# Three units of an expert layer's first product computed by seven half-size products

## The chip, the cores and the metric

One core of one Trainium2 chip runs the kernel. The metric is device time in microseconds (us) of one execution. TensorE (PE) multiplies matrices into PSUM, VectorE (DVE) and ScalarE (ACT) read PSUM and work elementwise, GpSimd (POOL) copies and issues transfers, SyncE (SP) issues transfers. Each engine carries out its own list of instructions in order and waits on semaphores for the others.

## The reference

Attention with a relative-position bias for 8 batches of 8 heads, 576 positions and 64 channels, and then a two-layer network with a squared ReLU on the 4608 tokens that it gives:

```python
scores = scale * np.matmul(q, k.transpose(0, 1, 3, 2)) + bias   # bias_table[bucket], per head
attn = softmax(scores)                                          # over the keys
x = (attn @ v).transpose(0, 2, 1, 3).reshape(B * S, H * D)      # 4608 x 512
h = np.maximum(x @ w_in, 0.0)                                   # w_in: 512 x 2048
out = h * h @ w_out                                             # w_out: 2048 x 512
```

All inputs and the output are fp32; the kernel multiplies in fp16 and accumulates in fp32.

## The kernel before

The kernel makes a list of operations, each with its engines, what it depends on, the ring buffers it takes and a due time (`P.add`), and a planner (`Plan.schedule`) puts them in order by its own cost figures. The order in which the planner lists them is each engine's program order; what an instruction waits for on the chip is then set by the tiles it reads and writes.

The work is of two kinds. **Attention** runs over 32 pairs of heads (`pair`): four score matmuls into the two double-bank PSUM tiles `st` (L702, with L726 and L751 for the last 64 queries and keys), exponentials on ACT from there into a `pt` buffer (L713), a table product on DVE (L794), the product with v into the one PSUM tile `pv` (L830, L837) in two parts, its normalisation on DVE into `x` (L854, L859), and a transposing transfer on SP's queue that puts `x` into `xt` with channels on the partitions (L875). **The two layers** run over nine groups of 512 tokens (`layers`). Layer 1 of a group is 16 tiles, one for each 128 of the 2048 hidden channels: four matmuls of 512 columns over the four 128-channel parts of x into one of three PSUM tiles `f` (L1102), a ReLU on ACT into one of four `rt` buffers (L1123), a square on DVE into the group's `g` buffer (L1133). Layer 2 of a group is computed already by seven half-size products in place of eight (`second`, Winograd's variant of Strassen's scheme): sums of activations on DVE (L972), seven products of 16 matmuls of 256 columns each, issued as two halves of eight (L1017), sums with the products on DVE or a plain copy on ACT (L1045, L1051), and the output transfers on SP (L1073).

In the list a group's 16 layer-1 tiles are due 2000 apart, and the halves of the layer-2 products of the group before lie between them. Groups 7 and 8 take tokens of the last batch (7), so that their layer 1 comes after the last pair (31); after that pair there are no more scores, and the two `st` tiles, the `pt` buffers and the staging buffers of q and k (`stg`, shown as qs and ks) are no longer used. Group 8 has no group after it: its layer 2 is the end of the kernel.

Of the kernel before, what the change touches and what calls it, by code (L numbers as in the profile page):

```python
# [11 lines left out]
FP16 = mybir.dt.float16  # L12
EXPF = mybir.ActivationFunctionType.Exp
RELUF = mybir.ActivationFunctionType.Relu
COPYF = mybir.ActivationFunctionType.Copy
MULT = mybir.AluOpType.mult

# [8 lines left out]
GT = 512  # L26
# [13 lines left out]
SIX = 2  # L40
V_EARLY, V_HW = 18900.0, 2
LATE2 = 7000
T_POOL, T_DUE = 0, 0
ORDER = "k0 i0 q1 q0 v i1 o0 k1 i2 o1 o2 i3 o3"
HALF = GT // 2
# [135 lines left out]
def mm(n):  # L181
    return n / 2.4 + 2.5
# [6 lines left out]
def dve(n, rate=1.0, fix=160.0):  # L189
    return fix + n / (0.96 * rate)  # L190
# [3 lines left out]
def kernel(  # L194
# [13 lines left out]
    def io(ins):  # L208
        tc.keep_in_program_order(ins)
        return ins  # L210
# [399 lines left out]

    xt_ready, x_last = {}, {}
    x_bufs = {}

    def copy_to(engs_n, out_f, in_f, deps, bufs, due, fp16=True, dve_only=False):

# [13 lines left out]
    def pair(p):  # L629
# [63 lines left out]
        def run(jts):  # L693
            sets = [Buf(r_set) for _ in jts]

            def score():
                kt, qt = kts[qb.slot], qts[qb.slot]
                for jt, st in zip(jts, sets):
                    for e in range(2):
                        rw = ds(64 * e, 64)  # L700
                        io(
                            nc.tensor.matmul(  # L702
                                sets_ps[st.slot][:, e, :], kt[rw, ts(jt, 128)], qt[rw, 0:512],
                                start=True, stop=True,
                            )
                        )

            o = P.add({"PE": len(jts) * mm(512) + 10}, score, evac, sets + [qb, pb], T, after, "r")
            for jt, st in zip(jts, sets):

                def ex(jt=jt, st=st):
                    io(
                        nc.scalar.activation(  # L713
                            out=p5(pts[pb.slot])[:, jt, :, 0:512], in_=sets_ps[st.slot], func=EXPF, scale=SCALE
                        )
                    )

                exps[jt] = P.add({"ACT": act(1024)}, ex, [o], [st, pb], T)
# [214 lines left out]
    def sums_of_weights():  # L933
# [21 lines left out]
            done.append(o)  # L955
        return done

    def sums_of_activations(g):

        gb = g_bufs[g]  # L960
        sb_ = s_bufs[g] = {i: Buf(r_s[i]) for i in (1, 2, 4)}
        for c0 in (0, 4):
            o = None
            for to, uses in ((1, [1]), (2, [1, 2]), (4, [2, 4]), (3, [])):

                def add(to=to, c0=c0):
                    a11, a12, a21, a22 = (fourth(gb, eo, t, c0, 4) for t in range(2) for eo in range(2))
                    s = {i: ss[i][:, c0 : c0 + 4] for i in (1, 2, 4)}
                    out_, a, b_ = {
                        1: (s[1], a21, a22), 2: (s[2], a11, s[1]), 4: (s[4], a12, s[2]), 3: (a21, a21, a11)  # L970
                    }[to]
                    io(nc.vector.tensor_tensor(out=out_, in0=a, in1=b_, op=mybir.AluOpType.subtract))  # L972

                o = P.add(
                    {"DVE": dve(1024, 2.0)}, add, squares[g][2 * c0 : 2 * c0 + 8] + [o],
                    [gb] + [sb_[i] for i in uses], G0 + GP * g - 5e4,
                )
                s_done.setdefault((g, to), []).append(o)

    def second(g):  # L980
# [25 lines left out]
        for i in (int(x) for x in (P_LAST if g == NG - 1 else P_ORDER).split()):  # L1006
            bk, left, right, ns = prod[i]
            own = bk == "e" and g == NG - 1
            home = pv_ps if own else g_ps
            apart = bk == "d" and g == NG - 1  # L1010
            for s_ in range(2):
                bf = bank[f"d{s_}" if bk == "d" else bk]

                def mul(i=i, s_=s_, bf=bf, left=left, right=right, apart=apart, own=own, home=home):
                    for c in range(8):
                        io(
                            nc.tensor.matmul(  # L1017
                                home[bf.slot][:, ts(s_, HALF)], left(c, s_), right(c),
                                start=(c == 0 and (s_ == 0 or apart) and (own or i not in before)), stop=(c == 7),
                                skip_group_check=True,  # L1020
                            )
                        )

                def atom(d, i=i, s_=s_, bf=bf, ns=ns, mul=mul, own=own):
                    deps = d + [x for n in ns for x in s_done[g, n]] + squares[g]
                    deps += read_of[before[i]] if i in before and not own else []
                    deps += l_wout if i in (1, 2) else t_done
                    return P.add(
                        {"PE": 8 * mm(HALF)}, mul, deps, [bf, gb] + [sb_[n] for n in ns if n != 3], 1e6, 0.0, "f",
                    )  # L1030

                atoms.append(atom)
                if s_ == 0 and not apart:
                    continue

                def fin(o, i=i, bf=bf, s0=s_ if apart else 0, n=1 if apart else 2, own=own, home=home):
                    to, plus, where = reads[i]
                    plus = "u" if own else plus
                    cs = ds(s0 * HALF, n * HALF)

                    def ev():
                        dst, ps = ys[y[to].slot][:, cs], home[bf.slot][:, cs]
                        if plus is not None:
                            io(
                                nc.vector.scalar_tensor_tensor(  # L1045
                                    out=dst, in0=ps, scalar=OSC, in1=ys[y[plus].slot][:, cs], op0=MULT,
                                    op1=mybir.AluOpType.add,
                                )
                            )
                        elif e.eng == "ACT":  # L1050
                            io(nc.scalar.activation(out=dst, in_=ps, func=COPYF, scale=OSC))  # L1051
                        else:
                            io(nc.vector.tensor_scalar_mul(out=dst, in0=ps, scalar1=OSC))

                    deps = [o]
                    if plus == "u":
                        deps += read_of[1 if i in (2, 6) else 6]
                    if i == 6 and g == NG - 1:
                        deps += read_of[2]
                    if plus == "v":  # L1060
                        deps += read_of[5]
                    if i == 4:
                        deps += read_of[3] + read_of[5]
                    bufs = [bf, y[to]] + ([y[plus]] if plus not in (None, to) else [])
                    engs = {"DVE": dve(n * HALF)} if plus is not None else {"DVE": dve(n * HALF), "ACT": act(n * HALF)}
                    e = P.add(engs, ev, deps, bufs, 0.0)
                    read_of.setdefault(i, []).append(e)
                    if where is not None:
                        t, h = where
                        P.add(  # L1070
                            {"SP": 640.0},
                            lambda: io(
                                nc.sync.dma_start(  # L1073
                                    out=rows_[t][:, s0 : s0 + n, ts(h, HALF)],
                                    in_=ys[y[to].slot][:, cs].rearrange("p (s d) -> p s d", s=n),
                                )
                            ),
                            [e], [y[to]], 0.0,
                        )

                atoms.append(fin)
        return atoms

    def layers(g):

        due = G0 + GP * g
# [2 lines left out]
        if g < NG:  # L1089
            g_bufs[g] = Buf(r_gb)  # L1090
            gb1 = g_bufs[g]
            squares[g] = []
            for nt in range(16):
                bank = Buf(r_g)

                def f1(nt=nt, bank=bank):
# [10 lines left out]
                            )  # L1107

                atoms1.append((nt, f1, bank))
        i2 = 0  # L1110
        last = None
        for i in range(16):
            if i < len(atoms1):
                nt, f1, bank = atoms1[i]
                o = P.add(
                    {"PE": 4 * mm(512)}, f1, xt_ready[g] + [l_win[nt // 4]], [bank, gb1], due + i * 2000, 0.0, "f"
                )
                f1_last[g] = o
                rb = Buf(r_rt)
# [1 line left out]
                def relu(o, bank=bank, rb=rb):  # L1121
# [4 lines left out]

                engs = {"ACT": act(512), "DVE": dve(512)} if g < RELU_DVE else {"ACT": act(512)}
                r = one_of(engs, relu, [o], [bank, rb], 0.0)
                squares[g].append(
                    P.add(  # L1130
                        {"DVE": dve(512, 2.0)},
                        lambda rb=rb, nt=nt, gb1=gb1: io(
# [64 lines left out]
```

## Time and profile before

| what | value |
|---|---|
| median of 7 runs | 373.34 us (372.69 to 374.43) |
| the profiled execution's own time | 373.06 us |
| its span, first to last instruction | 371.2 us |
| ACT busy, 300-310 / 310-315 / 315-320 us | 4.43 / 0.00 / 2.26 us |
| DVE busy, 300-310 / 310-315 / 315-320 us | 7.05 / 2.81 / 1.91 us |
| DVE busy, 320-325 / 325-330 / 330-335 us | 3.05 / 4.11 / 4.36 us |
| DVE busy, 335-340 / 340-345 / 345-350 / 350-355 us | 1.36 / 1.88 / 3.34 / 2.83 us |
| layer-1 matmuls of groups 7 and 8 | 314.13 us to 355 us |
| last matmuls begin | 366.21 us |

A profile is of one execution. In a timeline each line is a start, a length, the engine, the line of the kernel, the operation, what it writes and reads, the shape and the count of merged instructions; in brackets the idle time of the engine before it and what ended that. The page's slices cut the span into 40; a digit is the busy share in tenths. Matmuls are pipelined, so that the length of one is longer than the distance to the next.

### The profile page before, as it was taken

What the parts mean: (1) busy time and instruction counts of PE and PEld (TensorE: products, weight loads), DVE (VectorE), ACT (ScalarE), POOL (GpSimd) and SP (SyncE); (2) the same over time, 40 slices, a digit from 0 to 9 for tenths busy, and PEclk for the clock granted to TensorE, in tenths of its full rate; (3) what the DMA queues carried; (4) which work ended last, traced back from release to release, by engine and by line L of the source; (5) the groups of instructions that cost most, each with busy time, mean ns of one, the idle gap of its engine ahead of it and who ended that gap; (6) DMA issues with size and microseconds to landing.
All of it is one profiled execution on the core that took longest, in us unless ns stands there. A gap on an engine that the chain in (4) does not pass through costs nothing.

```text
span 371.2 us, 9910 instructions
## 1 busy us (share of the span) xinstructions
PE 355.2 (96%) x3930; PEld 242.4 (65%) x3930; DVE 265.1 (71%) x594; ACT 257.5 (69%) x367; POOL 188.2 (51%) x343
## 2 busy tenths in 40 slices
PE   3988999899999999999999999999999999999996
PEld 2756455556587457877785467745876688546785
DVE  3997789967775598668865787579765885583573
ACT  4998989688576887679766887688659870564220
POOL 7898349494665687668755655677623100000000
PEclk9999999999999999999999999999999999999999
DMA  9999999895999999999999799999975112200022
GB/s 166 151 133 160 201 179 87 108 112 99 174 127 127 149 161 116 150 164 156 116 132 148 115 140 133 135 170 142 121 107 130 48 44 57 78 2 28 30 85 87
DMA packets 162292, 44.25 MB, mean 119 GB/s; under 512 B 145734, under 2 KB 162246, under 8 KB 162246
## 3 DMA queue, kind: packets, MB, share of 16 engines
q0 software_dynamic: 74208, 14.53, 50.4%
q1 hardware_dynamic: 87696, 28.80, 41.0%
q8 instruction: 31, 0.51, 0.6%
q10 hardware_dynamic: 342, 0.30, 0.3%
q14 instruction: 15, 0.12, 0.1%
HBM read 36.88 MB, written 9.44 MB: 125 GB/s over the span
## 4 chain that ended last, share of the span: by engine, by line
PE 86%; DVE 7%; DMA 3%; ACT 2%; issue 1%; POOL 0%; SPq 0%; ACTq 0%; DVEq 0%
PE f L1102 34%; PE f L1017 28%; PE pv L837 8%; PE st L702 8%; PE pv L830 2%; PE st L751 2%; DVE pt L794 2%; DMA kt<-ks 2%; PE st L726 1%; DVE x L859 1%; DMA g<-in_q_dram 1%; PE f L657 1%; ACT pm L761 1%; DVE s L972 1%; PE f L359 1%
## 5 line engine op out<-in xcount | busy, mean ns | idle before, releaser
L713 ACT ACTIVATE pt<-st 128x1024 f16<-128x1024 f32 x128 | 127.4, 1024 | 30.7 <-PE st L702 30.7
L1102 PE MATMUL f<-xt,w_in_sb 128*128 128x512 f16 (+4 forms) x704 | 138.5, 341 | 0.2 <-ACT xt L619 0.2
L1123 ACT ACTIVATE rt<-f 128x512 f16<-128x512 f32 x144 | 85.2, 601 | 49.2 <-PE f L1102 44.0
L1102 PEld LDWEIGHTS <-w_in_sb 128*128 128x128 f16 x704 | 62.5, 98 | 57.3 <-issue 12.2
L1133 DVE TENSOR_TENSOR g<-rt 128x512 f16<-128x512 f16 x144 | 64.0, 449 | 36.3 <-ACT rt L1123 35.1
L794 DVE TENSOR_TENSOR pt<-pt,tb_sb 128x1536 f16<-128x1536 f16 (+2 forms) x96 | 60.6, 641 | 14.7 <-ACT pt L713 14.0
L1017 PEld LDWEIGHTS <-g 128*128 128x128 f16 x576 | 54.5, 98 | 14.4 <-issue 4.7
L276 POOL DMA_DIRECT2D qs<-in_q_dram x79 | 55.4, 714 | 7.4 <-DMA w_in_sb<-in_moe_w_in_dram 2.5
L276 POOL DMA_DIRECT2D ks<-in_k_dram x79 | 55.3, 702 | 1.1 <-issue 1.0
L837 PE MATMUL pv<-va,pt 128*128 128x65 f16 x1280 | 54.7, 193 | 0.0
L837 PEld LDWEIGHTS <-pt 128*128 128x128 f16 x1280 | 50.2, 97 | 3.2 <-issue 1.3
L1045 DVE SCALAR_TENSOR_TENSOR y<-f,y 128x512 f32<-128x512 f32 (+1 forms) x47 | 31.4, 667 | 23.1 <-PE f L1017 22.7
L1017 PEld LDWEIGHTS <-s 128*128 128x128 f16 x432 | 41.2, 98 | 9.8 <-issue 2.5
L702 PE MATMUL st<-qt,kt 64*128 64x512 f16 x256 | 40.5, 387 | 0.9 <-ACT pt L736 0.4
L684 POOL COPY qz<-kt 64x64 f16<-64x64 f16 x58 | 21.1, 364 | 38.8 <-DMA kt<-ks 31.9
L830 PE MATMUL pv<-vm,pm 128*128 128x130 f16 x160 | 35.3, 221 | 1.1 <-DVE x L859 1.0
L1017 PE MATMUL f<-wt,g 128*128 128x256 f16 x288 | 36.2, 273 | 0.0
L1017 PE MATMUL f<-w_out_sb,s 128*128 128x256 f16 x288 | 36.1, 273 | 0.0
L684 POOL COPY qz<-qt 64x64 f16<-64x64 f16 x61 | 18.4, 302 | 33.1 <-DMA qt<-qs 29.7
L1017 PE MATMUL f<-w_out_sb,g 128*128 128x256 f16 x272 | 34.5, 273 | 0.7 <-ACT y L1051 0.7
L859 DVE TENSOR_TENSOR x<-pv,r 128x384 f16<-128x384 f32 x64 | 31.4, 491 | 2.0
L972 DVE TENSOR_TENSOR s<-g,s 128x1024 f16<-128x1024 f16 x36 | 25.1, 698 | 0.4
(66 smaller groups left out, 285.7 us busy)
## 6 DMA issues: line engine op xcount, KB each, us to landing
out_dram<-y SPq DMA_DIRECT2D x34, 256.0 KB, 2.3
f<-in_v_dram SPq DMA_DIRECT2D x24, 256.0 KB, 4.2
qs<-in_q_dram POOLq DMA_DIRECT2D x48, 64.0 KB, 4.3
ks<-in_k_dram POOLq DMA_DIRECT2D x48, 64.0 KB, 3.7
w_in_sb<-in_moe_w_in_dram POOLq DMA_DIRECT2D x4, 512.0 KB, 8.9
w_out_sb<-in_moe_w_out_dram POOLq DMA_DIRECT2D x4, 512.0 KB, 12.8
qs<-in_q_dram POOLq DMA_DIRECT2D x7, 144.0 KB, 4.3
ks<-in_k_dram POOLq DMA_DIRECT2D x7, 144.0 KB, 6.7
```

Source lines behind the costliest of these rows:

```text
L276: lambda: io(eng.dma_start(out=out_(), in_=in_())),
L684: io(eng.tensor_copy(out=dst[qb.slot][rw, rw], in_=src[qb.slot][rw, 512:576]))
L702: nc.tensor.matmul(sets_ps[st.slot][:, e, :], kt[rw, ts(jt, 128)], qt[rw, 0:512], start=True, stop=True,)
L713: nc.scalar.activation(out=p5(pts[pb.slot])[:, jt, :, 0:512], in_=sets_ps[st.slot], func=EXPF, scale=SCALE)
L794: io(nc.vector.tensor_tensor(out=a, in0=a, in1=t, op=MULT))
L830: nc.tensor.matmul(ps[:, i, :, :], pm[:, c : c + 128], vm[:, hp, :, 0:65], start=True, stop=False)
L837: nc.tensor.matmul(ps[:, i, e, :], pt[:, (2 * jt + e) * S + c : (2 * jt + e) * S + c + 128], va[:, jt, 2 * hp + e, 0:65], start=False, sto ...
L859: nc.vector.tensor_tensor(out=xs[xb.slot][:, qt0 : qt0 + nq, :].rearrange("p t (e d) -> p t e d", e=2), in0=ps[:, :, :, 0:64], in1=rs[rb.s ...
L1017: nc.tensor.matmul(home[bf.slot][:, ts(s_, HALF)], left(c, s_), right(c), start=(c == 0 and (s_ == 0 or apart) and (own or i not in before ...
L1102: nc.tensor.matmul(g_ps[bank.slot][:, a:z], w_in_sb[:, kk, ts(nt, 128)], xt_sb[:, kk, c : c + z - a], start=(kk == 0), stop=(kk == 3),)
L1123: io(nc.scalar.activation(out=rts[rb.slot], in_=g_ps[bank.slot], func=RELUF))
L1133: nc.vector.tensor_tensor(out=gs[gb1.slot][:, nt, :], in0=rts[rb.slot], in1=rts[rb.slot], op=MULT)
```

## The change

`UNITS` names two units of group 7 and one of group 8. A unit is four layer-1 tiles: hidden channels 256u to 256u + 255 and 1024 + 256u to 1024 + 256u + 255. They are no longer computed tile by tile. `by_sevens` takes the block of w_in and the group's part of xt as 2x2 blocks (halves of the hidden channels, halves of the 512 input channels, halves of the 512 tokens) and computes the four result blocks by seven products of four matmuls of 256 columns, in place of eight. Products 1, 6, 2 go to one `st` tile (1 and 2 to its first bank, 6 to its second), 5, 7, 3, 4 to the other (5 and 3 to the first, 7 and 4 to the second). ACT copies product 1 to an fp32 buffer (one of the two `f32` buffers), DVE adds the others to what has been made so far, from PSUM; the four results go through ReLU (on ACT) and square (on DVE or ACT) into `g`.

The sums of blocks of xt (four for each group) are made on DVE into staging buffers; the sums of blocks of w_in (four for each unit u, made once) on DVE into a `pt` buffer, with the scores of the last pair as something they depend on and the due time of group 7. The other tiles of the group get due times between those of the seven products (`place`, `AT`). The list `squares` is kept by tile, so that a sum of activations depends on its own tiles.

```diff
+UNITS = {7: 2, 8: 1}
+
+AT = (0, 0.5, 2, 2.5, 4, 5.5, 7)
...
+    last_scores = []
             o = P.add({"PE": len(jts) * mm(512) + 10}, score, evac, sets + [qb, pb], T, after, "r")
+            if p == 4 * B - 1:
+                last_scores.append(o)
...
+    def made(g, a, z):
+
+        return [x for nt in range(a, z) for x in squares[g][nt]]
-                    {"DVE": dve(1024, 2.0)}, add, squares[g][2 * c0 : 2 * c0 + 8] + [o],
+                    {"DVE": dve(1024, 2.0)}, add, made(g, 2 * c0, 2 * c0 + 8) + [o],
-                    deps = d + [x for n in ns for x in s_done[g, n]] + squares[g]
+                    deps = d + [x for n in ns for x in s_done[g, n]] + made(g, 0, 16)
...
+    def sum_of_w(i, u):
+        return pts[late["room"].slot][:, ts(i - 1, 1024)].rearrange("p (k c) -> p k c", k=2)[:, :, ts(u, 256)]
...
+    def by_sevens(g, units, due):
...
+
+            late["room"] = Buf(r_pt)
+        wq = lambda i, k, u: w_in_sb[:, 2 * k : 2 * k + 2, 1024 * i + 256 * u : 1024 * i + 256 * u + 256]
+        xq = lambda k, j: xt_sb[:, 2 * k : 2 * k + 2, c + HALF * j : c + HALF * j + HALF]
+        o_ = 4 * (g - min(UNITS)) - 1
+        t = lambda i: stg[(i + o_) // 2][(i + o_) % 2][:, 0:512].rearrange("p (k c) -> p k c", k=2)
+        t_ops = late_sums(
+            512, t,
+            [
+                (1, (lambda: xq(0, 1), lambda: xq(0, 0), SUB)),
+                (2, (lambda: xq(1, 1), lambda: t(1), SUB)),
+                (4, (lambda: xq(1, 0), lambda: t(2), SUB)),
+                (3, (lambda: xq(1, 1), lambda: xq(0, 1), SUB)),
+            ],
+            xt_ready[g], due - 1e5,
+        )
+        gb1 = g_bufs[g]
...
+        for u in range(units):
+            s_ = lambda i, u=u: sum_of_w(i, u)
+            if ("ops", u) not in late:
+                late["ops", u] = late_sums(
+                    512, s_,
+                    [
+                        (1, (lambda u=u: wq(1, 0, u), lambda u=u: wq(1, 1, u), mybir.AluOpType.add)),
+                        (2, (lambda s_=s_: s_(1), lambda u=u: wq(0, 0, u), SUB)),
+                        (4, (lambda u=u: wq(0, 1, u), lambda s_=s_: s_(2), SUB)),
+                        (3, (lambda u=u: wq(0, 0, u), lambda u=u: wq(1, 0, u), SUB)),
+                    ],
+                    l_win + last_scores, due + 10.0 * u, [late["room"]],
+                )
+            sets = {"ab": Buf(r_set), "cd": Buf(r_set)}
+            y = {"u": Buf(r_f), "v": Buf(r_y)}
+            at = lambda i, y=y: (fs if i == "u" else ys)[y[i].slot]
+            prod = {
+                1: ("a", lambda u=u: wq(0, 0, u), lambda: xq(0, 0), True),
+                6: ("b", lambda s_=s_: s_(2), lambda: t(2), True),
+                2: ("a", lambda u=u: wq(0, 1, u), lambda: xq(1, 0), False),
+                5: ("c", lambda s_=s_: s_(1), lambda: t(1), True),
+                7: ("d", lambda s_=s_: s_(3), lambda: t(3), True),
+                3: ("c", lambda s_=s_: s_(4), lambda: xq(1, 1), False),
+                4: ("d", lambda u=u: wq(1, 1, u), lambda: t(4), False),
+            }
+            reads = {
+                1: ("u", None, None), 6: ("u", "u", None), 2: (None, None, (0, 0)), 5: ("v", "u", None),
+                7: (None, "v", (1, 1)), 3: (None, "u", (0, 1)), 4: (None, "u", (1, 0)),
+            }
+            after_read = {2: 1, 3: 5, 4: 7}
+            read_of = {}
+            for n, i in enumerate((1, 6, 2, 5, 7, 3, 4)):
+                bk, left, right, first_ = prod[i]
+                st = sets["ab" if bk in "ab" else "cd"]
+                ps = lambda st=st, bk=bk: sets_ps[st.slot][:, "abcd".index(bk) % 2, :]
+
+                def mul(left=left, right=right, first_=first_, ps=ps):
+                    for f in range(2):
+                        for kk in range(2):
+                            io(
+                                nc.tensor.matmul(
+                                    ps()[:, ts(f, HALF)], left()[:, kk, ts(f, 128)], right()[:, kk, :],
+                                    start=(first_ and f == 0 and kk == 0), stop=(kk == 1), skip_group_check=True,
+                                )
+                            )
+
+                o = f1_last[g] = P.add(
+                    {"PE": 4 * mm(HALF)}, mul,
+                    xt_ready[g] + t_ops + late["ops", u] + (read_of[after_read[i]] if i in after_read else []),
+                    [st, gb1, late["room"]], due + (8 * u + AT[n]) * 2000.0, 0.0, "f",
+                )
+                to, plus, where = reads[i]
+                deps = [o]
+                if plus == "u":
+                    deps += read_of[1 if i == 6 else 6]
+                if plus == "v":
+                    deps += read_of[5]
+                bufs = [st] + [y[x] for x in {to, plus} - {None}]
+                rb = Buf(r_rt) if where else None
+                bufs += [rb] if rb else []
+
+                def ev(e, to=to, plus=plus, ps=ps, at=at, rb=rb):
+                    dst = rts[rb.slot] if rb else at(to)
+                    if plus is not None:
+                        io(
+                            nc.vector.scalar_tensor_tensor(
+                                out=dst, in0=ps(), scalar=1.0, in1=at(plus), op0=MULT, op1=mybir.AluOpType.add
+                            )
+                        )
+                    else:
+                        io(nc.scalar.activation(out=dst, in_=ps(), func=RELUF if rb else COPYF))
+
+                e = one_of({"DVE": dve(512) + 100.0} if plus else {"ACT": act(512) + 100.0}, ev, deps, bufs, 0.0)
+                read_of[i] = [e]
+                if not rb:
+                    continue
+                if plus is not None:
+                    e = P.add(
+                        {"ACT": act(512)},
+                        lambda rb=rb: io(nc.scalar.activation(out=rts[rb.slot], in_=rts[rb.slot], func=RELUF)),
+                        [e], [rb], 0.0,
+                    )
+
+                def square(o, rb=rb, where=where, u=u):
+                    src = rts[rb.slot].rearrange("p (f s) -> p f s", f=2)
+                    n0 = 8 * where[0] + 2 * u
+                    dst = gs[gb1.slot][:, n0 : n0 + 2, ts(where[1], HALF)]
+                    if o.eng == "ACT":
+                        io(nc.scalar.activation(out=dst, in_=src, func=SQUAREF))
+                    else:
+                        io(nc.vector.tensor_tensor(out=dst, in0=src, in1=src, op=MULT))
+
+                e = one_of({"DVE": dve(512, 2.0), "ACT": act(512)}, square, [e], [rb, gb1], due - 1e5)
+                for f in range(2):
+                    squares[g][8 * where[0] + 2 * u + f].append(e)
...
-            squares[g] = []
-            for nt in range(16):
+            squares[g] = {nt: [] for nt in range(16)}
+            units = UNITS.get(g, 0)
+            for nt in [nt for nt in range(16) if nt % 8 >= 2 * units]:
                 bank = Buf(r_g)
                 atoms1.append((nt, f1, bank))
+            if units:
+                by_sevens(g, units, due)
+
+            def place(d):
+                return 2 * d + 1 if d < 4 * units else 4 * units + d
+
+        skip = 16 - len(atoms1) if g < NG else 0
-            if i < len(atoms1):
-                nt, f1, bank = atoms1[i]
+            if i >= skip and g < NG:
+                nt, f1, bank = atoms1[i - skip]
                 o = P.add(
-                    {"PE": 4 * mm(512)}, f1, xt_ready[g] + [l_win[nt // 4]], [bank, gb1], due + i * 2000, 0.0, "f"
+                    {"PE": 4 * mm(512)}, f1, xt_ready[g] + [l_win[nt // 4]], [bank, gb1], due + place(i - skip) * 2000,
+                    0.0, "f",
                 )
...
-                squares[g].append(
+                squares[g][nt].append(
```

More of the change, by code (lines that the diff above doesn't have):

```diff
@@ L14 @@
 RELUF = mybir.ActivationFunctionType.Relu
+SQUAREF = mybir.ActivationFunctionType.Square
 COPYF = mybir.ActivationFunctionType.Copy
@@ L1082, in second, with late_sums @@
         return atoms
+    late = {}
+    def sum_of_w(i, u):
+        return pts[late["room"].slot][:, ts(i - 1, 1024)].rearrange("p (k c) -> p k c", k=2)[:, :, ts(u, 256)]
+    def late_sums(n, dst, terms, deps, due, bufs=()):
+        o, made_ = None, []
+        for i, (a, b_, op) in terms:
+            o = P.add(
+                {"DVE": dve(n, 2.0)},
+                lambda i=i, a=a, b_=b_, op=op: io(nc.vector.tensor_tensor(out=dst(i), in0=a(), in1=b_(), op=op)),
+                deps + [o], bufs, due,
+            )
+            made_.append(o)
+        return made_
@@ new lines @@
+    SUB = mybir.AluOpType.subtract
+    def by_sevens(g, units, due):
+        assert max(UNITS.values()) <= 2
+        if not late:
+            late["room"] = Buf(r_pt)
+        c = (g * GT) % XR
+        assert c + GT <= XR
+        wq = lambda i, k, u: w_in_sb[:, 2 * k : 2 * k + 2, 1024 * i + 256 * u : 1024 * i + 256 * u + 256]
[90 more added lines that the diff above has]
+                        [e], [rb], 0.0,
+                    )
+                def square(o, rb=rb, where=where, u=u):
[9 more added lines that the diff above has]
+                    squares[g][8 * where[0] + 2 * u + f].append(e)
```

## The prediction

> **What bounds the kernel now.** I read the page's busy and slice rows first, then the timelines of TensorE (PE), VectorE (DVE) and ScalarE (ACT) over the last 75 us, where the edit lies.
>
> ```profile
> PE 355.2 (96%) x3930; PEld 242.4 (65%) x3930; DVE 265.1 (71%) x594; ACT 257.5 (69%) x367; POOL 188.2 (51%) x343
> PE   3988999899999999999999999999999999999996
> ...
> PEclk9999999999999999999999999999999999999999
> ```
>
> The page's busy rows and slices: PE is full to the last slice, at full clock.
>
> ```profile
> 315.87 1.89 PE L1102 MATMUL f<-xt,w_in_sb 128*128 128x512 f16 x8
> 317.60 1.04 PE L1017 MATMUL f<-wt,g 128*128 128x256 f16 x8
> 318.47 14.84 PE L1102 MATMUL f<-xt,w_in_sb 128*128 128x512 f16 x68
> 333.15 1.04 PE L1017 MATMUL f<-w_out_sb,g 128*128 128x256 f16 x8
> 334.02 1.03 PE L1102 MATMUL f<-xt,w_in_sb 128*128 128x512 f16 x4
> 334.88 1.04 PE L1017 MATMUL f<-w_out_sb,g 128*128 128x256 f16 x8
> ...
> 366.21 1.91 PE L1017 MATMUL f<-wt,g 128*128 128x256 f16 x16
> ```
>
> PE's timeline (start, length, instruction; durations run past the next start, so only differences of starts count). From 296 us on there is no gap. 68 matmuls of 512 columns take 333.15 - 318.47 = 14.68 us: 0.8635 a layer-1 tile of four. Eight of 256 columns take 0.873 (333.15 to 334.02): four would take 0.4365. So here a microsecond of matmul saved or lost is one of the end, if PE stays full.
>
> ```profile
> 314.13 1.03 PE L1102 MATMUL f<-xt,w_in_sb 128*128 128x512 f16 x4
> 315.00 1.04 PE L1017 MATMUL f<-wt,g 128*128 128x256 f16 x8
> 315.20 0.60 ACT L1123 ACTIVATE rt<-f 128x512 f16<-128x512 f32 x1 [9.34 <-PE f L1102]
> 315.83 0.43 DVE L1133 TENSOR_TENSOR g<-rt 128x512 f16<-128x512 f16 x1 [0.80 <-ACT rt L1123]
> ```
>
> All engines, the first tile of group 7: its matmuls give way at 315.00, ACT starts at 315.20 (hand-over 0.20), ends at 315.80, DVE starts at 315.83 (0.03).
>
> ```profile
> 314.33 0.69 DVE L1045 SCALAR_TENSOR_TENSOR y<-f,y 128x512 f32<-128x512 f32 x1 [1.06 <-PE f L1017]
> 18.59 0.56 DVE L859 TENSOR_TENSOR x<-pv,r 128x384 f16<-128x384 f32 x1
> 19.20 0.22 PE L830 MATMUL pv<-vm,pm 128*128 128x130 f16 x1 [0.35 <-DVE x L859]
> ```
>
> A sum with a product read from PSUM takes DVE 0.69. DVE ends at 19.15 and the PE that waited starts at 19.20 (0.05). These five numbers price every wait below.
>
> **Part 1, the matmuls.** A unit drops four tiles, 4 x 0.8635 = 3.454, and adds seven products of four 256-column matmuls, 7 x 0.4365 = 3.056. Gain 0.40 a unit, 1.20 for three, all on the bounding engine.
>
> A rule speaks against it. The Trainium skill (TensorE: Matmul & The Clock Gate, Back-to-back issue gap) puts the sustained cost of a 512-column matmul with its weight load at about 131 ns, against 81 at 128 columns. By it a unit's 16 wide matmuls cost 2.10 us and 28 narrow ones 2.27 to 3.67, a loss. The rows above say 216 and 109 ns, and they decide.
>
> **Part 2, waits that PE gets.** The built order and its semaphores decide this. The products go to the two-bank score tiles st: 1, 6 and 2 to one, 5, 7, 3 and 4 to the other. The waits built are on the whole tile, not on the bank: a later product waits until every earlier one in its tile has been read, and a read waits for every earlier write. PE's order, with T a regular tile: unit one 1 6 5 7 2 T T 3 4; unit two 1 6 T 2 5 7 T 3 T 4; group 8's unit 1 6 5 7 2, half a layer-2 product, T, 3 4. Each wait is the chain of readers less the PE work placed between:
> - Unit one, product 2: ACT may copy product 1 only after 6 is written, then DVE adds 6, then PE goes on: 0.20 + 0.60 + 0.03 + 0.69 + 0.05 = 1.57. Between stand 5 and 7, 0.87. PE idles 0.70.
> - Unit two, product 3: after 7, DVE reads 5, then 7: 0.20 + 0.69 + 0.03 + 0.69 + 0.05 = 1.66; one T between, 0.86. Idle 0.80.
> - Unit two, product 4 behind the read of 3: 0.20 + 0.69 + 0.05 = 0.94 less 0.86: 0.08.
> - Group 8, product 3: after 2, DVE reads 6, 5 and 7: 0.20 + 3 x 0.69 + 0.06 + 0.05 = 2.38, less 0.873 + 0.8635: 0.64.
> - The other product 2s wait 0.20 + 0.60 + 0.05 = 0.85 behind 0.86 or 0.87: nothing, by 0.01. Unit one's 3 and 4 have two T before them: nothing.
>
> Sum 2.22 us. Queued behind the waiting product are all later matmuls, and nothing can overtake in PE's order, so the idle time isn't refilled.
>
> The bounds: if dependent DVE sums follow each other as the page's unlinked ones do (288.46 after 287.85, 0.61 apart), each step loses 0.08, the sum is 2.22 - 0.08 x 7 = 1.66. If every hand-over costs twice its row, four chains of about 0.3 add 1.1: 3.3. I take 2.2, since each step is the row itself.
>
> **Part 3, work beside PE.** A unit takes four ACT relus (0.60) and four DVE squares (0.43) away and gives DVE five sums (0.69), ACT five copies or relus, and four squares to either. DVE also gets eight sums of w_in and, per group, four of xt, 128x512 halves; the nearest row is the square, 0.43, the bounds 0.415 (the 2x256 band product at 300.02) and 0.69 (twice the width). In all DVE gets 15 x 0.69 + 16 x 0.43 - 6 x 0.43 = 14.7 us, ACT about 15 x 0.60 + 6 x 0.60 - 12 x 0.60 = 5.4.
>
> The w_in sums (3.4) lie between 303 and 313 us, where DVE was busy 7.05 of 10 in 300-310 and 2.81 of 5 in 310-315. They stand in front of pair 31's normalisations. By the built order PE does layer 2 in runs of 16 matmuls between the pv parts; pair 31's first norm ends at about 311.1 and its bank is wanted at 311.8. Without that 0.7 of cover the loss would be what the sums exceed it by; at 0.69 each the one sum just ahead adds 0.3, still covered.
>
> On SP the transposes of x are re-ordered: pair 31's second part now stands behind an output whose sum ends at about 315.0, so it goes at 315.7 instead of 314.65. Landing took up to 4.1, so 319.8; DVE wants it for group 8 at about 322. Its first part, now behind pair 30's second, goes at 311.1, lands by 315.2, and the first T's fourth matmul wants it at 316.5. Nothing on PE, with 1.3 and more to spare; POOL's queue is unchanged.
>
> ACT squares and ACT relus from SBUF are not in the trace. Bounds: 0.60 (512 from PSUM) and 0.84 (L477, 768 fp32 from SBUF); I take 0.60, the same size. At 0.60 the relus of the T behind unit two free their banks 0.2 to 0.25 before PE wants them. At 0.84 one of them is 0.25 late. No table load is added.
>
> **Sum.** 2.22 - 1.20 = +1.0 us, the last matmul moving with it: what follows it (last sum, output) is as before. The profiled run was 373.06 (span 371.2 and 1.86 around it): 374.06. The median of the runs shown is 0.28 above that run, so the forecast is 374.3.
>
> **Clock.** Idles of 0.7 us could cost more if PE slowed after them. At the start twelve 96-column transposes took 0.69 us after 6.09 idle (6.09 us) and 0.45 at 18.08, after an idle of 0.47 at 16.40. So half a microsecond costs no clock; longer ones are not shown late in the kernel.
>
> The skill's same page (Why this matters for your kernels) puts the limit at PE gaps of about 3 us, which would leave these idles at their own length. No run here tests it.
>
> **Rivals.**
> 1. Forecast: the four waits stand open and outweigh the columns. 374.3, by its own bounds 373.8 (1.66 idle) to 375.4 (3.3). Chance 0.55.
> 2. The waits are half covered: sums overlap, hand-overs are shorter because the profile's ends of matmuls are modelled. Idle 1.2 to 1.6, gain eaten: 373.5. For: DVE's 0.61 spacing. Against: each sum needs the one before, and L854 to L859 show 0.03 after the end. Chance 0.24.
> 3. Faster: nothing waits, 373.34 - 1.20 = 372.1. The mechanism is the columns alone; it decides if PE's idle stays under 0.45 us, which needs a DVE step of about 0.3 in unit two (0.86 - 0.28 over two). Against: 0.69 in every row. A read that waits on its bank alone isn't what was built. Chance 0.08.
> 4. ACT and DVE pile up behind unit two: 0.25 more per late bank, up to three T, and product 2 of unit two by as much: 374.3 + 1.0 = 375.3. For: DVE gets 11 us more in the 40 after 315, where it was busy 23. Chance 0.11.
> 5. PE's clock falls after an idle: at 0.69 for 0.45, four microseconds of matmul cost about 2 more: 376.3. Chance 0.02.
>
> **Numbers.** A measurement tells no change within about 0.2%, 0.75 us. Slower by more: 0.42 of the forecast's 0.55, and rivals 4 and 5: 0.55 and a little of rival 2, 0.60. Faster: rival 3 and a little of 2, 0.10. The same: 0.30. The range 373.0 to 375.6 leaves out rival 3, rival 5 and the ends of 4; the likeliest case alone has 373.8 to 375.4.
>
> **What would show it.** Right: PE idle before the new products, 0.7, 0.8 and 0.6 us, released by DVE sums, some 2.2 in all; matmul time 1.2 less; the first group-7 tile at about 315.9. Wrong: no PE gap from 316 to 335 (rival 3), PE waiting for regular tiles' banks (4), four-matmul products over 0.44 after a gap (5), or a late first tile (the w_in sums or SP's order).

## The result, and the profile after

The changed kernel took 374.8 us in the median of 14 runs (374.06 to 377.23), the kernel before 373.04 in 35 runs beside it: a ratio of 1.0053, 95% interval [1.0039, 1.0068]. A second set of the same kernel gave 1.0032 [1.0011, 1.0053]. It is slower, by 0.3 to 0.5%. The profiled execution took 375.86, its span is 374.1. One execution of a later version (told, layer 2 later) had a granted clock of 0.855 and took 413.23 us; it is in no ratio below, and its profile gives no stretch to compare.

The page's busy rows and slices of the changed kernel:

```profile
PE 355.3 (95%) x3966; PEld 246.0 (66%) x3966; DVE 277.1 (74%) x620; ACT 261.1 (70%) x375; POOL 185.6 (50%) x343
...
PE   3988999899999999999999999999999999999996
...
PEclk9999999999999999999999999999999999999999
```

In tenths nothing is to be seen: PE still looks full to the last slice, at full clock. The idle time shows in the PE timeline of the changed kernel (start, length, engine, line, what it writes and reads; in brackets the idle time and what ended it):

```profile
317.24 2.75 PE L1254 MATMUL f<-xt,w_in_sb 128*128 128x512 f16 x12
319.82 0.60 PE L1179 MATMUL st<-xt,w_in_sb 128*128 128x256 f16 x4
320.26 0.60 PE L1179 MATMUL st<-ks,pt 128*128 128x256 f16 x4
320.70 1.04 PE L1179 MATMUL st<-qs,pt 128*128 128x256 f16 x8
322.32 0.60 PE L1179 MATMUL st<-xt,w_in_sb 128*128 128x256 f16 x4 [0.59 <-DVE f L1204]
322.76 1.89 PE L1254 MATMUL f<-xt,w_in_sb 128*128 128x512 f16 x8
...
328.44 1.03 PE L1254 MATMUL f<-xt,w_in_sb 128*128 128x512 f16 x4
330.31 0.60 PE L1179 MATMUL st<-xt,pt 128*128 128x256 f16 x4 [0.84 <-DVE rt L1204]
330.74 1.03 PE L1254 MATMUL f<-xt,w_in_sb 128*128 128x512 f16 x4
331.75 0.60 PE L1179 MATMUL st<-ks,w_in_sb 128*128 128x256 f16 x4
...
339.57 1.03 PE L1254 MATMUL f<-xt,w_in_sb 128*128 128x512 f16 x4
341.16 0.60 PE L1179 MATMUL st<-xt,pt 128*128 128x256 f16 x4 [0.56 <-DVE rt L1204]
```

The group at 319.82 is product 1 of unit one, then come 6, and 5 and 7 together; at 322.32 comes product 2. Eight narrow matmuls fill 0.87, but 322.32 lies 1.62 after 320.70: PE idles 0.75. (The bracket counts from the modelled end of the last matmul, which is later, so it says less.) In the same way 330.31 - 328.44 - 0.86 = 1.01 ahead of unit two's product 3, 331.75 - 330.74 - 0.86 = 0.15 ahead of its product 4, and 341.16 - 339.57 - 0.86 = 0.73 ahead of group 8's product 3: 2.64 in all. A sum on DVE ended each of the three large ones. (Another 0.04, ahead of unit two's product 2, is left out.) The kernel before has no such idle after its last scores.

All engines of the changed kernel around the first wait:

```profile
320.95 0.60 ACT L1209 ACTIVATE f<-st 128x512 f32<-128x512 f32 x1 [0.33 <-PE st L1179]
...
321.58 0.69 DVE L1204 SCALAR_TENSOR_TENSOR f<-st,f 128x512 f32<-128x512 f32 x1 [0.50 <-ACT f L1209]
322.32 0.60 PE L1179 MATMUL st<-xt,w_in_sb 128*128 128x256 f16 x4 [0.59 <-DVE f L1204]
```

Product 1 gave way to product 6 at 320.26, but ACT, idle for 0.33, copies it only at 320.95, 0.25 after product 6 gave way at 320.70. Product 2 is added onto product 1 in its bank, which ACT left at 321.55, but starts at 322.32, 0.05 after the end of the sum that reads product 6 from the other bank. So both waits are on the tile, not on the bank. A version with one tile for each bank was not run; what it would gain is not shown.

How much of the 375.86 is the change's? The first and the last PE group of the closing stretch, before and then after:

```profile
304.83 0.39 PE L726 MATMUL st<-qz,kt 128*128 128x128 f16 x4
```

```profile
306.19 0.39 PE L733 MATMUL st<-qz,kt 128*128 128x128 f16 x4
...
369.04 1.91 PE L1028 MATMUL f<-wt,g 128*128 128x256 f16 x16
```

Before, from the last scores at 304.83 to the last group at 366.21, there are 61.38 us; after, 62.85: +1.47, which is 2.64 of idle less 1.17. The remaining 1.36 of the profiled difference lies before that. The scores at 301.64 before start at 303.00 after, so all of it is there ahead of the change's first instruction, a sum of w_in on DVE at 305.36, and until then the engines' orders are the same in both kernels; it isn't the change's. Why the two executions differ there is open. The ratio's interval, 1.45 to 2.54 us (0.0039 and 0.0068 of 373.04), and that of the second set, 0.4 to 2.0, both hold 1.47.

### The profile page after: what moved, and what is told of

It reads as the page before. It is cut to its first block, busy times and chain, and to the rows that moved or that the text cites. A ratio compares the mean times of both kernels' runs of the same rounds, so it can differ in the third digit from the quotient of the medians.

```text
span 374.1 us, 10023 instructions
## 1 busy us (share of the span) xinstructions
PE 355.3 (95%) x3966; PEld 246.0 (66%) x3966; DVE 277.1 (74%) x620; ACT 261.1 (70%) x375; POOL 185.6 (50%) x343
## 4 chain that ended last, share of the span: by engine, by line
PE 82%; DVE 8%; DMA 5%; ACT 2%; issue 1%; POOL 0%; SPq 0%; DVEq 0%; ACTq 0%
PE f L1254 30%; PE f L1028 27%; PE st L707 8%; PE pv L844 8%; DMA kt<-ks 4%; PE st L1179 2%; PE pv L837 2%; PE st L758 2%; DVE pt L801 2%; PE st L733 1%; DVE x L866 1%; DMA g<-in_q_dram 1%; PE f L662 1%; ACT pm L768 1%; DVE f L1204 1%
## 5 line engine op out<-in xcount | busy, mean ns | idle before, releaser
L1254 PE MATMUL f<-xt,w_in_sb 128*128 128x512 f16 (+4 forms) x656 | 127.3, 338 | 0.2 <-ACT xt L624 0.2
L1283 ACT ACTIVATE rt<-f 128x512 f16<-128x512 f32 x132 | 77.7, 601 | 34.8 <-PE f L1254 30.6
L1254 PEld LDWEIGHTS <-w_in_sb 128*128 128x128 f16 x656 | 57.9, 98 | 52.7 <-issue 12.2
L1293 DVE TENSOR_TENSOR g<-rt 128x512 f16<-128x512 f16 x132 | 57.0, 439 | 21.6 <-ACT rt L1283 20.5
```

What stands on the lines that cost most here:

```text
L1254: nc.tensor.matmul(g_ps[bank.slot][:, a:z], w_in_sb[:, kk, ts(nt, 128)], xt_sb[:, kk, c : c + z - a], start=(kk == 0), stop=(kk == 3),)
L1283: io(nc.scalar.activation(out=rts[rb.slot], in_=g_ps[bank.slot], func=RELUF))
L1293: nc.vector.tensor_tensor(out=gs[gb1.slot][:, nt, :], in0=rts[rb.slot], in1=rts[rb.slot], op=MULT)
```

## The experiments

Below, "stretch" runs from the start of the last 64-query score matmul to that of the last matmul of the kernel (62.85 before, 64.32 after). Each is 1.47 longer than the distance between the two groups' starts above; that this equals the loss, and that 62.85 stood there for the changed kernel, is chance. The stretch leaves out what varies in the 300 us before it. "Idle" is PE's, worked out as above, gaps over 0.06. A stretch is of one profile. Where there is a stretch, the ratio's interval holds what the difference of the stretches makes of it, but is too wide to tell the told versions apart; that rests on the stretches.

| run | ratio to before, 95% interval | stretch | idle |
|---|---|---|---|
| before | | 62.85 | 0 |
| the change | 1.0053 [1.0039, 1.0068] | 64.32 | 2.64 |
| the change, again | 1.0032 [1.0011, 1.0053] | 64.32 | 2.64 |
| sums alone | 1.0004 [0.9986, 1.0022] | 62.85 | 0 |
| group 8's unit alone | 1.0025 [1.0004, 1.0046] | 63.19 | 0.71 |
| one square moved | one execution | 64.19 | 2.51 |
| planner told | 0.9976 [0.9957, 0.9994] | 62.34 | 0.66 |
| told, group 7 alone | 0.9984 [0.997, 0.9997] | 62.06 | 0 |
| told, group 8 alone | 0.9992 [0.9975, 1.0008] | 62.45 | 0 |
| told, layer 2 later | 0.9966 [0.995, 0.9982] | not comparable | |
| told, layer 2 later, again | 0.9976 [0.9956, 0.9997] | 61.66 | 0 |
| before, layer 2 later | 0.9992 [0.9978, 1.0006] | 62.85 | 0 |

**The change again, unchanged.**

> The changed kernel unchanged, on the same chip as the others. Theory: 1.2 to 1.5 us more than before, PE idle 0.7 + 1.0 + 0.1 + 0.7 us between 316 and 345 us in this run too; of the first profile's 2.9 us of span, 1.4 came ahead of the first changed instruction and is not the change's. Rival (the idle lets the clock of PE fall in some executions): granted clocks below 1.0 in the slower executions of this kernel and none in those of the others.

The idles come out at the same four places and the same lengths, and the stretch is 64.32 again. What differs from one execution to the next lies ahead of it. Executions with a granted clock of about 0.995 occur here (4 of 12), but as well with the sums alone (5 of 12) and in the kernel before beside them (11 of 35), where PE has no such idle; so they don't come from the idles of the products.

**The planner told of the waits on the whole tile.**

```diff
-            after_read = {2: 1, 3: 5, 4: 7}
+            after_read = {2: (1, 6), 3: (5, 7), 4: (7, 3)}
...
-                    xt_ready[g] + t_ops + late["ops", u] + (read_of[after_read[i]] if i in after_read else []),
+                    xt_ready[g] + t_ops + late["ops", u] + [x for k in after_read.get(i, ()) for x in read_of[k]],
```

The instructions and their waits on the chip are of the same kinds; the planner only knows now when a product can start, and puts regular tiles ahead of it.

> The changed kernel with the planner told the waits that the two-bank tiles bring: product 2 is made to depend on the read of 6 as well as of 1, 3 on the reads of 5 and 7, 4 on those of 7 and 3, so that the planner puts regular tiles into the gaps. Same work, another order. Theory (the loss is PE idle behind these reads, 2.6 us in the profiled changed kernel, against 1.2 us of columns gained): no idle over 0.2 us ahead of the products, and about 1.2 us less than before, some 371.8 against 373.0, and 2.6 less than the changed kernel. Rival (DVE and ACT are too full in the tail, or the narrow products are slow): the idle only moves to the regular tiles' banks and the time stays at 374 or more.

All idle ahead of the products was gone, and the kernel was faster than the one before. But the stretch was 62.34, where 1.20 less than before would be 61.65: a new idle of 0.66 stood further on, in the first layer-2 product of group 8 that takes a sum of activations. All engines of this run there:

```profile
346.35 1.04 PE L1028 MATMUL f<-w_out_sb,g 128*128 128x256 f16 x8
...
346.61 0.60 ACT L1283 ACTIVATE rt<-f 128x512 f16<-128x512 f32 x1 [0.19 <-PE f L1254]
...
347.22 0.60 PE L1028 MATMUL f<-wt,s 128*128 128x256 f16 x4
347.24 0.42 DVE L1293 TENSOR_TENSOR g<-rt 128x512 f16<-128x512 f16 x1 [0.36 <-ACT rt L1283]
347.58 1.41 DVE L983 TENSOR_TENSOR s<-g,s 128x1024 f16<-128x1024 f16 x2
...
348.32 1.49 PE L1028 MATMUL f<-wt,s 128*128 128x256 f16 x12 [0.50 <-DVE s L983]
```

The last layer-1 tile gave way at 346.35. With its ReLU, its square and one sum behind it, PE goes on at 348.32, 1.97 later, and had twelve narrow matmuls, 1.31, to do meanwhile. The regular tiles that now cover the products no longer stand early: the last of them comes too late for the sums.

**The same, with more of group 7's layer 2 behind the last tile.** The edit above and

```diff
-LATE2 = 7000
+LATE2 = 9000
```

> The planner is told the waits of the whole st tile, as in the first run of that kind, and group 7's layer-2 halves that lie in group 8's stage are due 2000 later (LATE2 9000 in place of 7000), so that more of them stand between the last layer-1 tile and the first product that needs a sum of activations. My theory (the change's columns are worth 1.20, and only waits eat them): PE shows no idle of 0.1 us or more after the last scores, the stretch from the last 64-query scores to the last matmul is 62.85 - 1.20 = 61.65, and the ratio to before is about 0.997. Rival (the narrow matmuls cost more than half a wide one, or the work that DVE and ACT get must come out somewhere): the stretch stays at about 62.3 as in the first such run, with idle time somewhere else.

The times came as expected (0.9966); without a stretch to compare, the idle stayed open. The same kernel again:

> The same kernel as the run with the planner told and LATE2 9000, for an undisturbed profile and a second interval. My theory: no idle of 0.1 us or more, the stretch from the last 64-query scores to the last matmul 61.65 (62.85 - 1.20), ratio 0.9965 to 0.997. Rival (the lower times of the first run came from its mixture of executions and not from the stretch): stretch 62.0 or more and a ratio of 0.998 or above.

PE's timeline of this second run, group 8's last products to the first products with sums:

```profile
340.47 1.04 PE L1028 MATMUL f<-w_out_sb,g 128*128 128x256 f16 x8
341.34 0.60 PE L1179 MATMUL st<-xt,pt 128*128 128x256 f16 x4
341.78 1.04 PE L1028 MATMUL f<-w_out_sb,g 128*128 128x256 f16 x8
342.65 1.03 PE L1254 MATMUL f<-xt,w_in_sb 128*128 128x512 f16 x4
343.51 0.60 PE L1179 MATMUL st<-ks,w_in_sb 128*128 128x256 f16 x4
343.95 1.91 PE L1028 MATMUL f<-w_out_sb,g 128*128 128x256 f16 x16
345.70 1.89 PE L1254 MATMUL f<-xt,w_in_sb 128*128 128x512 f16 x8
347.42 1.91 PE L1028 MATMUL f<-wt,s 128*128 128x256 f16 x16
349.17 1.91 PE L1028 MATMUL f<-w_out_sb,s 128*128 128x256 f16 x16
```

No bracket is left: each start follows the one before by 0.44 for four narrow matmuls, 0.86 for a tile, 1.75 for sixteen narrow ones. The stretch is 61.66, that is 1.19 shorter than before, and this version beats both kernels: 0.2 to 0.3% under the kernel before. The ratio of this second set came out at 0.9976, nearer the rival's 0.998 than the 0.9965 to 0.997 that were expected; it is the stretch that speaks against the rival. The profile has a mean clock of 0.994, and the drop lies far ahead of the stretch (window, its length, then busy time of PE, PEld, DVE, ACT and POOL with the instructions, then the granted clock, the share of the DMA and GB/s):

```profile
22.70:26.10 3.40, 1.94 (x30) 1.24 (x29) 3.23 (x16) 3.40 (x6) 3.22 (x8) 1.00 1.62 117
26.10:29.50 3.40, 3.40 (x54) 2.36 (x51) 2.68 (x8) 2.43 (x3) 3.09 (x6) 0.50 1.49 88
29.50:368.00 338.50, 333.91 (x3567) 231.42 (x3565) 254.33 (x551) 237.53 (x345) 159.96 (x295) 1.00 0.91 116
```

**Is it the due time alone?** The kernel before with LATE2 = 9000:

> The kernel before with LATE2 9000 alone. Mine: no idle and nothing gained, the stretch from the last 64-query scores to the last matmul 62.85 as before, ratio 1.000. Rival (the due time alone is worth something): a stretch below 62.6.

The stretch stays at 62.85. The due time by itself gains nothing; the gain is the products'.

**Group 7's two units alone, told** (`UNITS = {7: 2}` and the edit of `after_read`):

> Only the two units of group 7, the planner told the waits of the whole tile, LATE2 as it was. My theory: no idle of 0.1 us or more ahead of a product; the stretch from the last 64-query scores to the last matmul 62.85 - 0.80 = 62.05, ratio 0.998. It sizes a unit: with the other told run 0.40 for each. Rival (a unit is worth less than 0.40, since narrow matmuls fill less well): the stretch 62.3 to 62.5 without any idle time.

62.06 and no idle: 0.79 for two units. With group 8's unit, 1.19: 0.40 for each.

**Group 8's unit alone, not told** (`UNITS = {8: 1}`):

> One unit, of group 8 alone. The built order has a regular tile between product 6 and 2 and three between 7 and 3, so that every chain of reads is covered. Theory: no idle ahead of the products and 0.4 us less than before, some 372.6 against 373.0. Rival (a unit costs time by itself, whatever its place): 0.3 us or more slower than before, a third of the change's loss.

This missed: the stretch grew by 0.34. All engines:

```profile
331.69 0.60 PE L1179 MATMUL st<-qs,pt 128*128 128x256 f16 x4
331.95 0.69 DVE L1204 SCALAR_TENSOR_TENSOR f<-st,f 128x512 f32<-128x512 f32 x1 [0.48 <-PE st L1179]
...
332.13 1.03 PE L1254 MATMUL f<-xt,w_in_sb 128*128 128x512 f16 x4
332.56 0.42 DVE L1293 TENSOR_TENSOR g<-rt 128x512 f16<-128x512 f16 x1
...
332.89 0.69 DVE L1204 SCALAR_TENSOR_TENSOR y<-st,f 128x512 f32<-128x512 f32 x1
...
333.63 0.60 PE L1179 MATMUL st<-qs,pt 128*128 128x256 f16 x4 [0.47 <-DVE y L1204]
```

Product 5 is at 331.69, then a tile, then 7 at 333.63. With the unit alone the planner set one tile between 5 and 7, which share a tile but no bank. So 7 waited for the read of 5, and that stood in DVE's order behind the read of 6 and a square. 333.63 - 332.13 - 0.86 = 0.64 of idle, 0.07 more later, less the unit's 0.40, makes 0.31 of the 0.34; 0.04 ahead of product 2 makes the rest, within rounding. I had looked for the waits that the changed kernel has, and not for those that another order of the same products gets.

**The same, told:**

> Only group 8's unit, with the planner told the waits of the whole tile, so that no product of a tile is put between another product of it and that one's read without tiles to cover it. In the untold run of group 8's unit, product 7 idled 0.64 behind the read of product 5 and product 4 0.07. My theory: that idle was the same whole-tile wait; with it told, no idle of 0.1 or more, the stretch from the last 64-query scores to the last matmul 62.85 - 0.40 = 62.45, ratio 0.999. Rival (group 8's unit is late by its DVE work, whatever the order): idle of 0.3 or more stays and the stretch is 62.8 or more.

5 and 7 stand together again, there is no idle, and the stretch is 62.45. So the late product was the order's doing and not DVE's load.

**The sums alone.** The sums of w_in and of xt are made and not used; all 16 tiles of each group are computed as before.

> Only the sums of the change: the eight sums of w_in and the four of xt for each of groups 7 and 8 are made and not used, all 16 tiles of each group are computed as before. Theory: they lie beside PE's work, within 0.3 us of before. Rival (the sums delay pair 31's normalisations or the transfers behind them): 0.5 us or more slower, with a PE gap ahead of group 7's first tile.

No idle, the stretch to 0.01 that of before: the sums cost nothing. What they add to DVE's work shows in the windows of before and then of this run (columns as above):

```profile
300.00:310.00 10.00, 10.00 (x156) 8.87 (x155) 7.05 (x17) 4.43 (x7) 0.00 (x0) 1.00 0.23 55
```

```profile
300.00:310.00 10.00, 10.00 (x156) 8.88 (x155) 8.59 (x21) 4.19 (x6) 0.00 (x0) 1.00 0.26 61
```

DVE goes from 7.05 to 8.59 of 10, and PE stays at 10.00.

**One square moved.** In unit two's longest wait a square stood between the reads of 6 and 5 in DVE's order. Here it goes behind the read of 7; it then reads its buffer after the next result has been written there, so that this block of `g` isn't the reference's.

```diff
+                if (g, u, i) == (7, 1, 7):
+                    late["read"] = e
...
+                if (g, u, i) == (7, 0, 7):
+                    late["square"] = e
...
-    for op in P.schedule():
+    ops = list(P.schedule())
+    ops.remove(late["square"])
+    ops.insert(ops.index(late["read"]) + 1, late["square"])
+    for op in ops:
```

> The changed kernel with one square of unit one (that of its product 7) put behind unit two's reads of products 5 and 7 in DVE's order; nothing else moves. The first profile had 1.01 of idle ahead of unit two's product 3 where 0.80 was predicted. Theory A (the square is in the way, and the hand-over from PE is 0.27 in place of 0.20): the idle falls to about 0.87. Theory B (the reads themselves take longer behind one another): it stays at 1.0. Either way the other idles stay at 0.75 and 0.73, and that of product 4 at 0.15 to 0.3.

DVE and PE in the changed kernel, and then with the square moved:

```profile
327.83 0.69 DVE L1204 SCALAR_TENSOR_TENSOR f<-st,f 128x512 f32<-128x512 f32 x1 [0.98 <-PE st L1179]
...
328.44 1.03 PE L1254 MATMUL f<-xt,w_in_sb 128*128 128x512 f16 x4
328.44 0.41 DVE L1229 TENSOR_TENSOR g<-rt 128x512 f16<-128x512 f16 x1
328.77 0.69 DVE L1204 SCALAR_TENSOR_TENSOR y<-st,f 128x512 f32<-128x512 f32 x1
...
329.56 0.69 DVE L1204 SCALAR_TENSOR_TENSOR rt<-st,y 128x512 f16<-128x512 f32 x1
```

```profile
326.90 1.03 PE L1258 MATMUL f<-xt,w_in_sb 128*128 128x512 f16 x4
...
327.11 0.69 DVE L1204 SCALAR_TENSOR_TENSOR y<-st,f 128x512 f32<-128x512 f32 x1
...
327.90 0.69 DVE L1204 SCALAR_TENSOR_TENSOR rt<-st,y 128x512 f16<-128x512 f32 x1
...
328.64 0.60 PE L1179 MATMUL st<-xt,pt 128*128 128x256 f16 x4 [0.71 <-DVE rt L1204]
```

The read of 5 now starts 0.21 after product 7 gave way (327.11 - 326.90) in place of 0.33, and the idle is 0.88 in place of 1.01. So the square cost 0.13. Theory A's other half is refuted here: the hand-over was 0.21 and not 0.27, and its 0.87 came out by luck. What is left over the predicted 0.80 is mostly the step from one read to the next, 0.79 in place of 0.72; why that step was longer here is open.

## Why the prediction was right, and where its size was off

The direction and the mechanism were right: the columns saved less than what four waits on whole tiles cost. The stretch lengthened by 1.47 where +1.0 was predicted; the term that was mis-sized is Part 2. The predicted +1.0 lies below the first set's interval (1.45 to 2.54) and inside the second's (0.4 to 2.0).

- **Part 1, 0.40 a unit and 1.20 for three.** Measured 1.19 once the idle was gone, 0.79 for two, 0.40 for one. The Trainium skill's sustained figures (TensorE: Matmul & The Clock Gate, Back-to-back issue gap: 131 ns for a 512-column matmul, 81 ns for 128 columns) had made it a loss by the prediction's estimate; the runs side with the 216 and 109 ns of the rows. The formula that the same section gives for a single matmul, N / 2.4 + 2.5 ns, comes to an estimate of 216 and 109 ns for 512 and 256 columns: here it is this one that holds in a long sequence too, 14.68 us for 68 wide matmuls.
- **Part 2, the waits, 2.22 us in all.** Measured 2.64: 0.75 for 0.70, 1.01 for 0.80, 0.15 for 0.08, 0.73 for 0.64. The places were as predicted, the releaser too where the trace names one (the three large waits), and no other product waited by more than 0.04. Half of the miss is unit two's product 3, where the sum had no square between the two reads of DVE; the built order has one, of unit one's product 7, and it cost 0.13 of the 0.21. The remaining parts are hand-overs: from PE to a reader 0.25 to 0.27 in three of the chains, where the first tile's row had said 0.20, and 0.79 from a read to the next in unit two, where 0.72 had been added up (in group 8's chain it was 0.72 and 0.73, from 338.97 to 339.69 and 340.42). For product 4's chain the trace puts the 0.27 down to a ReLU on ACT and not to PE, so that one is less sure.
- **Part 3, nothing for the work beside PE.** Right in the sum: with the sums alone the stretch was unchanged, and the first group-7 tile came at 317.24, which is the predicted 315.9 plus the 1.36 that this execution was late already. ReLUs and squares on ACT from SBUF took 0.62 to 0.63, where 0.60 was taken. But Part 3 stopped at the layer-1 tiles. The sums of activations for group 8's layer 2 depend on the last tile, and as soon as the products were well placed, those were late by 0.66. In the changed kernel itself this cost nothing.
- **The sum.** 374.06 for the profiled run, measured 375.86: +0.47 from the stretch, the rest from ahead of the change. The ratios of the two sets come to +1.98 and +1.20 over before; the plain medians lie 1.76 and 0.67 apart.
- **Rivals.** Waits half covered: refuted, each was longer than its sum. Nothing waits: refuted for this order; it took the told order and the later layer 2. Pile-up behind unit two: no regular tile waited in the changed kernel. Clock: see the last section.

## What to carry to other kernels

In this kernel saved matmul work was worth its full length only once the engine's program order covered every new dependency, and what a product waited for was set by the tile as built, both banks of it, not by the data that it needs. Where a planner orders the work, tell it the waits that will really be built: here two edited lines turned the stretch's +1.47 into -0.51, and a due time, which alone gave nothing, brought the rest to -1.19. After such a gain, look at once for the next consumer of the work that was pushed back.

## What the runs showed of the hardware

- PE idles of 0.73 to 1.01 left the clock alone: the granted clock was 1.00 in every window from 300 us on, and the four narrow matmuls after the idle at 322.32 took 0.44 (to 322.76), as everywhere. That is within what the Trainium skill states (TensorE: Matmul & The Clock Gate, Why this matters for your kernels: no gaps above about 3 us); gaps near that limit did not occur here. But short idles don't rule a drop out: in the profile of the told kernel with layer 2 later, the granted clock was 0.50 from 26.1 to 29.5 us, and ahead of it, from the first matmul on, no matmul started more than 0.96 us after the one before it. PE was busy 1.94 of the 3.40 us ahead of it; in the kernel before it was busy 2.00 of the same 3.40, and the clock stayed at 1.00. What sets it off is open.
- Identical instruction streams differ by more than the effect looked for: the same first 300 us took 1.36 longer in one profile than in the other, both at a mean clock of 0.999 or more. The length of the changed stretch, in contrast, came out the same to 0.01 in two profiles of one kernel (64.32), and that made 0.4 us measurable.
